# The low halves of the softmax weights: GpSimd instead of VectorE, in an attention and MoE kernel

## The chip, the core and the metric

The kernel runs on one core of one Trainium2 chip. The core has TensorE (PE: matmuls, and PEld: its weight loads), VectorE (DVE), ScalarE (ACT) and GpSimd (POOL) as compute engines, SyncE (SP), which issues nearly all DMAs here, and 16 DMA engines. Each engine works through its own instruction stream in order; semaphores tie the streams together. The metric is the device time of one execution in microseconds.

## What is computed

A local-and-global attention with ALiBi distances, followed by a two-layer feed-forward stage with a tanh-like gate:

```python
def _attn_ref(q, k, v, n_global, n_local):
    B, H, S, D = q.shape                      # 4, 8, 768, 64
    scores = np.matmul(q, k.transpose(0, 1, 3, 2)) / np.sqrt(D)
    ...
    scores = np.where(keep, scores + bias, -1e9)   # 8 global keys, 96 local ones
    a = np.exp(scores - np.max(scores, axis=-1, keepdims=True))
    a = a / (np.sum(a, axis=-1, keepdims=True) + 1e-09)
    return np.matmul(a, v)

def _moe_ref(x, w_in, w_out):                 # 3072 x 512, 512 x 2048, 2048 x 512
    h = x @ w_in
    g = h * (1.0 / (1.0 + np.exp(-1.702 * h)))
    return g @ w_out
```

The inputs and the result are float32.

## The kernel before, in words

**Numbers in two halves.** Matmuls run in float16. Each float32 operand is split into a large half, its float16 rounding, and a small half, the float16 rounding of what remains; a product is then three float16 products (large x large, large x small, small x large). Splitting is a cast, most often on ScalarE, followed by a subtraction on VectorE.

**Attention.** The 3072 tokens are 24 blocks of 128. The first four blocks (the first of each sequence) go a way of their own (`first`). The other 20 go through `unit`, four units a block with two heads each, so there are 80 units. A unit computes, for 128 queries and the 232 keys that matter to them:

1. `scores` (L536): eight matmuls into the PSUM tile `s`;
2. `rows` (L542), once a head on VectorE: adds the mask, writes the scores to the SBUF tile `p` and the row maximum to `NM`;
3. the exponential (L552), once a head on ScalarE, in place in `p`;
4. the large half (L556): ScalarE casts `p`, 128x464, into the first half of the float16 tile `hl`;
5. the small half (L557): `p` minus the large half, into the second half of `hl`;
6. a DMA transpose from `hl` to `pt` (L558), issued by SyncE;
7. `values` (L567 to L569): twelve matmuls of `pt` with the values into the PSUM tile `pv`.

There are two `hl` tiles, two `p`, four `pt`, one `s`. So unit k+2 cannot cast before the transpose of unit k has read its `hl`, nor can its row step write `p` before the subtraction of unit k has read it, and the scores of the next unit wait until both row steps of the present one have read `s`. A block's four units end in `finish`, which divides by the row sums, splits the result (L697, L699) and transposes it by DMA (L700) into `xT`.

**The feed-forward stage** runs over chunks of two blocks. The first three chunks use `up` and `down`; the other nine use `up_two` and `down_two`, a Strassen-like scheme of seven products instead of eight (`product`, L827). The gate is a tanh on ScalarE (L859) and a multiply on VectorE (L860); the result is split again (L867 on ScalarE, L868 on VectorE) and multiplied by the second weights (`pile`, L895). While one chunk is in this stage, the units of later blocks are interleaved with it.

**What sets the order.** Nothing of the order is written by hand. Each step is a task with the engines that may run it, a cost in microseconds for each, the tasks it comes after, and the tiles it uses; many have a due time. `Work.order` goes through a model time and always gives a free engine the ready task that is due first, where the tiles are free; a task with costs for two engines (for example the output copy, L907 on VectorE or L908 on ScalarE, and the cast of L697) goes to the one that ends it sooner. Due times go back from a task to those before it by their costs, and a table of small corrections by task (`NUDGE`) is added. The result is one fixed order for each engine, DMAs on SyncE included. So a changed cost or engine in one task can change the order on every engine behind it.

The small half is `t5` in `unit`; its place among the engines and its cost are the first argument of `add`.

Of the kernel before, what the change touches and what calls it, by code (L numbers as in the profile page):

```python
# [36 lines left out]
SKIP = 24  # L37
# [50 lines left out]
class Work:  # L88
# [5 lines left out]
    def add(self, on, fn, after=(), bufs=(), want=1e9):  # L94
        t = Task(on, fn, [a for a in after if a is not None], bufs, want)
        t.tag = self.tag
        for a in t.after:
            a.next.append(t)
        for b in t.bufs:
            b.users.append(t)  # L100
        self.tasks.append(t)
        return t
# [107 lines left out]
def kernel(  # L210
# [11 lines left out]
    nc = tc.nc  # L222
# [61 lines left out]
    add = wk.add  # L284
# [234 lines left out]
    def unit(n, u, want_s, want_v):  # L519

        ns = 2
        W = ns * P - SKIP
        d = blk[n]
        before = prev.get(n, blk.get(n - 1))
        sp = Buf(r_s, [P, 2, W], F32, f"s{n}_{u}")
        pr = Buf(r_pr, [P, 2, W], F32, f"p{n}_{u}")
        pt = Buf(r_pt, [P, 4 * ns, P], F16, f"pt{n}_{u}")
        hs = (2 * u, 2 * u + 1)

        def scores(e):  # L530
            for j, h in enumerate(hs):
                for s in range(ns):
                    K = (before, d)[s]["QK"]()
                    for z in range(2):
                        lo, hi = (0, P - SKIP) if s == 0 else (P - SKIP, W)
                        nc.tensor.matmul(sp()[:, j, lo:hi], d["QK"]()[:, 0, h, :], K[:, 1 + z, h, P - (hi - lo):],  # L536
                                         start=(z == 0), stop=(z == 1), skip_group_check=True)

        def rows(e, j):
            h = hs[j]  # L540
            m = mm[:, h, 0:2].rearrange("p a c -> p (a c)")[:, SKIP:]
            nc.vector.tensor_tensor_reduce(out=pr()[:, j, :], in0=sp()[:, j, :], in1=m, scale=-1.0 / SC, scalar=3.0e38,  # L542
                                           op0=ALU.add, op1=ALU.min, accum_out=NM[:, n, h:h + 1])

        t1 = add({"PE": 4 * (2 * P - SKIP) / P * MM128}, scores, [*d["qk_ready"], *before["qk_ready"], *before["G"]],
                 [sp, d["QK"], before["QK"]], want_s)
        d.setdefault("S", []).append(t1)
        ex = []
        for j in range(2):
            t2 = add({"DVE": 0.365}, lambda e, j=j: rows(e, j), [t1, M2], [sp, pr])  # L550
            checks.append(t2)
            ex.append(add({"ACT": 0.473}, lambda e, j=j: nc.scalar.activation(  # L552
                pr()[:, j, :], pr()[:, j, :], AF.Exp, bias=NM[:, n, hs[j]:hs[j] + 1], scale=-1.0,
                accum_out=d["sm"]()[:, hs[j]:hs[j] + 1]), [t2], [pr, d["sm"]]))
        hl = Buf(r_hl, [P, 2, 2, ns * P], F16, f"hl{n}_{u}", lambda t: t.rearrange("p (z a w) -> p z a w", z=2, a=2))
        t4 = add({"ACT": 0.5}, lambda e: nc.scalar.copy(hl()[:, 0, :, SKIP:], pr()), ex, [pr, hl])  # L556
        t5 = add({"DVE": 0.55}, lambda e: nc.vector.tensor_sub(hl()[:, 1, :, SKIP:], pr(), hl()[:, 0, :, SKIP:]), [t4], [pr, hl])  # L557
        t6 = add({"SP": 0.7 * ns}, lambda e: nc.sync.dma_start_transpose(pt(), hl().rearrange("p a h w -> p (a h w)")),  # L558
                 [t5], [hl, pt])

        def values(e):
            for j, h in enumerate(hs):
                o = d["pv"]()[:, h]
                for s in range(ns):
                    V = (before, d)[s]["VR"]()
                    ph, pl = pt()[:, j * ns + s, :], pt()[:, (2 + j) * ns + s, :]
                    nc.tensor.matmul(o, ph, V[:, 0, h], start=(s == 0), stop=False, skip_group_check=True)  # L567
                    nc.tensor.matmul(o, ph, V[:, 1, h], start=False, stop=False, skip_group_check=True)  # L568
                    nc.tensor.matmul(o, pl, V[:, 0, h], start=False, stop=(s == ns - 1), skip_group_check=True)  # L569

        if u == 0:
            d["pv"] = Buf(r_pv, [P, H, D], F32, f"pv{n}")
        t7 = add({"PE": 6 * ns * MM64}, values, [t6, *d["v_ready"], *before["v_ready"], *before["VG"]],
                 [pt, d["pv"], d["VR"], before["VR"]], want_v)
        d.setdefault("V", []).append(t7)
        d.setdefault("exp", []).extend(ex)
# [366 lines left out]
    for n in range(NBLK):  # L943
        c = n // 2
        wk.tag = f"prep{n}"
        if n < FIRST:
            prep_first(n)
        else:
            prep(n)
        if n < EARLY:  # L950
            own_values(n)
        if n == EARLY:
            for j in range(2):
                clear(j)
        if n >= EARLY and place(n)[1] == 1:
            wk.tag = f"over{n}"
            handover(n)
        wk.tag = f"block{n}"
        if n < EARLY:
            first(n, 8.0 + 11.0 * n)  # L960
        else:
            for u in range(NU):
                ws_ = start[c, 0] - (60.0 if c < TWO else LEAD) + 5.2 * ((n % 2) * NU + u)
                unit(n, u, ws_, ws_ + 6.0)
        leading(n)
        wk.tag = f"x{n}"
        finish(n)
# [303 lines left out]
```

## Time and profile before

| | before |
|---|---|
| time, median of 3 runs | 601.39 us (601.16 to 601.64) |
| span of the profiled execution, first to last instruction | 600.7 us |
| busy time of TensorE | 587.5 us |
| busy time of VectorE | 503.0 us |
| busy time of ScalarE | 471.4 us |
| busy time of GpSimd | 5.8 us |

The profile is of one execution, whose span of 600.7 us is 0.7 us below the median of the runs; what lies around the span is no part of it. Rows of the profile name a line of the kernel, an engine, an operation, and tiles as output<-inputs with the buffer numbers left out; then partitions x elements, the count, the busy time, the mean duration of one in ns, and the idle time of the engine ahead of it with what ended it. Matmuls overlap in the pipeline, so their single durations are longer than their spacing.

GpSimd works only at the start, on constants, an identity and a few zeroed tiles; its last instruction there starts before 7 us.

### The profile page before, as it was taken

The numbers are of one execution on the slowest core, as the hardware profiler recorded it, in microseconds if no ns is written. First come the engines' busy times: TensorE is split into PE (matmuls) and PEld (weight loads), VectorE is DVE, ScalarE is ACT, GpSimd is POOL, SyncE is SP. The second block draws the span as 40 slices with busy tenths as digits, with TensorE's granted clock in tenths as the row PEclk, the third lists the DMA queues.
The fourth block names the chain that finished last, engine by engine and source line by source line (L and its number), as shares of the span: only waits on it lengthen the run. The fifth ranks groups of instructions, "written<-read, shape, count | busy, mean of one in ns | idle before, by whom it ended". The sixth has DMA issues, their size and how long they took to land.

```text
span 600.7 us, 17037 instructions
## 1 busy us (share of the span) xinstructions
PE 587.5 (98%) x6816; PEld 445.9 (74%) x6816; DVE 503.0 (84%) x1177; ACT 471.4 (78%) x1098; POOL 5.8 (1%) x18
## 2 busy tenths in 40 slices
PE   8989999999999999999999999999999999999996
PEld 5878767777777867777677777777678768867895
DVE  6998999999999999789699789798979978766532
ACT  3878899978768988888698899788999978944432
POOL 3000000000000000000000000000000000000000
PEclk9999999999999999999999999999999999999998
DMA  8998799999976768979996999999989999920001
GB/s 225 310 251 260 227 253 198 191 179 197 212 141 128 156 117 186 196 145 196 216 206 163 226 209 238 197 233 198 236 186 223 224 193 228 234 40 3 36 1 41
DMA packets 268502, 109.58 MB, mean 182 GB/s; under 512 B 249536, under 2 KB 250048, under 8 KB 268416
## 3 DMA queue, kind: packets, MB, share of 16 engines
q1 hardware_dynamic: 267984, 108.30, 86.6%
q8 instruction: 55, 0.90, 0.7%
q14 instruction: 31, 0.25, 0.1%
q10 hardware_dynamic: 432, 0.13, 0.1%
HBM read 57.67 MB, written 6.29 MB: 106 GB/s over the span
## 4 chain that ended last, share of the span: by engine, by line
PE 85%; DMA 7%; ACT 4%; DVE 2%; issue 1%; SPq 1%; POOL 0%; DVEq 0%; ACTq 0%; POOLq 0%
PE y L895 36%; PE pa L827 14%; PE h L787 10%; PE pb L827 10%; PE s L536 5%; DMA pt<-hl 3%; DMA QK<-QK 2%; PE s L604 1%; PE pv L567 1%; PE pv L569 1%; PE pv L568 1%; PE sT L623 1%; PE idle L1060 1%; DMA xT<-x 1%; DMA out_dram<-yo 1%
## 5 line engine op out<-in xcount | busy, mean ns | idle before, releaser
L895 PE MATMUL y<-w,g 128*128 128x512 f16 (+1 forms) x1248 | 266.8, 363 | 0.0
L895 PEld LDWEIGHTS <-g 128*128 128x128 f16 x1248 | 117.9, 98 | 103.3
L827 PEld LDWEIGHTS <-w 128*128 128x128 f16 x1728 | 101.3, 98 | 5.0
L552 ACT ACTIVATE p<-p,NM 128x232 f32<-128x232 f32 x160 | 76.4, 480 | 7.0 <-DVE NM L542 7.0
L827 PEld LDWEIGHTS <-T 128*128 128x128 f16 x1296 | 77.1, 98 | 6.0
L787 PE MATMUL h<-xT,w 128*128 128x256 f16 x576 | 69.4, 273 | 0.3 <-DMA xT<-x 0.2
L542 DVE CUSTOM_DVE_ANT_0 p<-s,mm 128x232 f32<-128x232 f32 x160 | 57.7, 395 | 8.2 <-PE s L536 7.3
L787 PEld LDWEIGHTS <-w 128*128 128x128 f16 x576 | 55.2, 98 | 9.3 <-issue 0.6
L557 DVE TENSOR_TENSOR hl<-p,hl 128x464 f16<-128x464 f32 x80 | 50.9, 636 | 10.2 <-ACT hl L556 10.1
L868 DVE SCALAR_TENSOR_TENSOR g<-t,g 128x512 f16<-128x512 f32 x72 | 49.3, 687 | 11.1 <-ACT g L867 10.9
L867 ACT ACTIVATE g<-t 128x512 f16<-128x512 f32 x72 | 45.0, 628 | 9.5 <-DVE t L860 8.1
L556 ACT CAST hl<-p 128x464 f16<-128x464 f32 x80 | 46.1, 576 | 6.4 <-DMA pt<-hl 4.4
L859 ACT ACTIVATE t<-h 128x512 f32<-128x512 f32 (+1 forms) x72 | 35.9, 515 | 18.2 <-DVE h L835 15.1
L835 DVE TENSOR_TENSOR h<-pb,h 128x256 f32<-128x256 f32 x72 | 29.6, 420 | 23.0 <-PE pb L827 19.6
L827 PE MATMUL pa<-xS,T 128*128 128x128 f16 x648 | 45.0, 219 | 0.0
L860 DVE SCALAR_TENSOR_TENSOR t<-t,h 128x512 f32<-128x512 f32 (+1 forms) x72 | 38.2, 553 | 4.6 <-ACT t L859 4.0
L536 PEld LDWEIGHTS <-QK 128*128 128x128 f16 x640 | 36.5, 98 | 3.7 <-DMA QK<-QK 0.2
L536 PE MATMUL s<-QK 128*128 128x128 f16 x320 | 38.4, 219 | 0.1
L827 PE MATMUL pb<-xS,w 128*128 128x128 f16 x540 | 37.5, 219 | 0.0
L567 PE MATMUL pv<-VR,pt 128*128 128x64 f16 x288 | 34.8, 193 | 2.6 <-DMA pt<-hl 2.6
L827 PE MATMUL pa<-xT,w 128*128 128x128 f16 x540 | 37.0, 219 | 0.0
L569 PE MATMUL pv<-VR,pt 128*128 128x64 f16 x288 | 34.8, 193 | 0.0
(181 smaller groups left out, 1079.9 us busy)
## 6 DMA issues: line engine op xcount, KB each, us to landing
ws<-in_moe_w_in_dram SPq DMA_DIRECT2D x8, 1024.0 KB
ws<-in_moe_w_out_dram SPq DMA_DIRECT2D x8, 1024.0 KB
raw<-in_q_dram SPq DMA_DIRECT2D x24, 256.0 KB
raw<-in_k_dram SPq DMA_DIRECT2D x24, 256.0 KB
out_dram<-yo SPq DMA_DIRECT2D x22, 256.0 KB
QK<-QK SPq DMA_DIRECT2D x40, 128.0 KB
raw<-in_v_dram SPq DMA_DIRECT2D x20, 256.0 KB
ws_00again<-in_moe_w_in_dram SPq DMA_DIRECT2D x8, 512.0 KB
```

The costliest lines, as they stand in the source:

```text
L536: nc.tensor.matmul(sp()[:, j, lo:hi], d["QK"]()[:, 0, h, :], K[:, 1 + z, h, P - (hi - lo):], start=(z == 0), stop=(z == 1), skip_group_che ...
L542: nc.vector.tensor_tensor_reduce(out=pr()[:, j, :], in0=sp()[:, j, :], in1=m, scale=-1.0 / SC, scalar=3.0e38, op0=ALU.add, op1=ALU.min, ac ...
L552: ex.append(add({"ACT": 0.473}, lambda e, j=j: nc.scalar.activation(pr()[:, j, :], pr()[:, j, :], AF.Exp, bias=NM[:, n, hs[j]:hs[j] + 1], ...
L556: t4 = add({"ACT": 0.5}, lambda e: nc.scalar.copy(hl()[:, 0, :, SKIP:], pr()), ex, [pr, hl])
L557: t5 = add({"DVE": 0.55}, lambda e: nc.vector.tensor_sub(hl()[:, 1, :, SKIP:], pr(), hl()[:, 0, :, SKIP:]), [t4], [pr, hl])
L567: nc.tensor.matmul(o, ph, V[:, 0, h], start=(s == 0), stop=False, skip_group_check=True)
L569: nc.tensor.matmul(o, pl, V[:, 0, h], start=False, stop=(s == ns - 1), skip_group_check=True)
L787: nc.tensor.matmul(ph()[:, fi, :], w1(s, cc, z, fi), X[:, y, cc, :], start=(j + cc == 0), stop=(j == 2 and cc == NCC - 1))
L827: nc.tensor.matmul(o()[:, fi], w, x()[:, y * NCC + 2 * k + cc, t], start=(first and fi + j + cc == 0), stop=(last and j + cc == 3), skip_g ...
L867: t4 = add({"ACT": 0.53}, lambda e, g=g, tt=tt: nc.scalar.mul(g()[:, 0], tt(), SG / (SX * SW)), u, [tt, g])
L868: t5 = add({"DVE": 0.61}, lambda e, g=g, tt=tt: nc.vector.scalar_tensor_tensor(g()[:, 1], tt(), SG / (SX * SW), g()[:, 0], ALU.mult, ALU.s ...
L895: nc.tensor.matmul(y(), part(zg, f), w2(s, z, f % 2)[:, m], start=(begin and f + j == 0), stop=(end and j == 2 and f == 2 * len(steps) - 1 ...
```

## The change

The subtraction that makes the small half is issued on GpSimd, and its task says so: it may run on GpSimd alone, at a planned cost of 1.1 where VectorE's was 0.55. The instruction has the same operands and shape.

```diff
-        t5 = add({"DVE": 0.55}, lambda e: nc.vector.tensor_sub(hl()[:, 1, :, SKIP:], pr(), hl()[:, 0, :, SKIP:]), [t4], [pr, hl])
+        t5 = add({"POOL": 1.1}, lambda e: nc.gpsimd.tensor_sub(hl()[:, 1, :, SKIP:], pr(), hl()[:, 0, :, SKIP:]), [t4], [pr, hl])
```

The order changes with it from the first unit on. In the rows below, tiles carry their numbers: `p4_1` and `s4_1` belong to block 4, unit 1; `hl0` and `hl1` are the two `hl` tiles; `wa` and `w` are weights being prepared, `qk165` the halves of queries and keys of block 5.

On VectorE, at the first two units, this stood before:

```order
L370 TENSOR_SCALAR wa6_0_1052<-ws6_0_923 128x1024
L557 TENSOR_TENSOR hl0_89<-p4_0_1024,hl0_89 128x2x232
L542 ISA p4_1_1064,NM_83<-s4_1_1043,mm_91 128x232
L542 ISA NM_83 128x1
L542 ISA p4_1_1064,NM_83<-s4_1_1043,mm_91 128x232
L542 ISA NM_83 128x1
L376 ISA wa6_0_1052<-wa6_0_1052,w6_0_1036 128x2048
L456 SCALAR_TENSOR_TENSOR qk165_0_1066<-raw5_961,qk165_0_1066 128x16x64
L376 ISA wa5_1_1003<-wa5_1_1003,w5_1_966 128x2048
L557 TENSOR_TENSOR hl1_90<-p4_1_1064,hl1_90 128x2x232
```

and this stands there now:

```order
L370 TENSOR_SCALAR wa6_0_1052<-ws6_0_923 128x1024
L376 ISA wa5_1_1003<-wa5_1_1003,w5_1_966 128x2048
L542 ISA p4_1_1079,NM_83<-s4_1_1043,mm_91 128x232
L542 ISA NM_83 128x1
L542 ISA p4_1_1079,NM_83<-s4_1_1043,mm_91 128x232
L542 ISA NM_83 128x1
L376 ISA wa6_0_1052<-wa6_0_1052,w6_0_1036 128x2048
L456 SCALAR_TENSOR_TENSOR qk165_0_1065<-raw5_961,qk165_0_1065 128x16x64
```

The two subtractions are gone from the stream, and a weight step (L376 of `wa5_1`) stands in the place of the first of them, three steps earlier than it stood.

On GpSimd the whole stream behind the start is now the 80 subtractions in the order of the units; it begins so:

```order
L414 MEMSET QZ3_163 64x4x128 x2
L557 TENSOR_TENSOR hl0_89<-p4_0_1024,hl0_89 128x2x232
L557 TENSOR_TENSOR hl1_90<-p4_1_1079,hl1_90 128x2x232
L557 TENSOR_TENSOR hl0_89<-p4_2_1121,hl0_89 128x2x232
L557 TENSOR_TENSOR hl1_90<-p4_3_1167,hl1_90 128x2x232
```

Nothing else of the program stands between them, so a subtraction there follows its cast or the subtraction before it.

On SyncE, around block 9, whose keys and queries are transposed by L458 (`QK9`), this stood before (L700 is the transpose of a finished block, L397 loads, L460 a copy within `QK`):

```order
L558 DMA_TRANSPOSE pt7_2_2141<-hl0_89 128x8x128
L458 DMA_TRANSPOSE QK9_2158<-qk169_0_2040 128x16x128
L700 DMA_TRANSPOSE xT3_2203<-x166_2087 128x8x128
L558 DMA_TRANSPOSE pt7_3_2215<-hl1_90 128x8x128
L397 DMA raw10_2261<-in_q_dram 128x8x64
L460 DMA QK9_2158<-QK9_2158 64x1024 x2
```

and this stands there now:

```order
L458 DMA_TRANSPOSE QK9_2139<-qk169_0_1981 128x16x128
L558 DMA_TRANSPOSE pt7_2_2196<-hl0_89 128x8x128
L558 DMA_TRANSPOSE pt7_3_2211<-hl1_90 128x8x128
L700 DMA_TRANSPOSE xT3_2225<-x166_2111 128x8x128
L460 DMA QK9_2139<-QK9_2139 64x1024 x2
L397 DMA raw10_2265<-in_q_dram 128x8x64
```

The key transpose has moved ahead of one unit's transpose, and the transpose of the finished block behind another's.

Counted over the whole program, VectorE loses its 80 subtractions; five output copies (L908 to L907), three casts (L697) and one weight step (L374 to L373) go from ScalarE to VectorE. TensorE's instructions are the same, in another order.

## The prediction

> **What bounds the kernel now.** I read the page's busy times first, then the stretches of 60 us, then TensorE's waits, and last the path of one unit (a pair of heads of one block: scores, row maxima, exponentials, their two halves, the DMA transpose, the product with the values).
>
> ```profile
> span 600.7 us, 17037 instructions
> PE 587.5 (98%) x6816; PEld 445.9 (74%) x6816; DVE 503.0 (84%) x1177; ACT 471.4 (78%) x1098; POOL 5.8 (1%) x18
> ```
>
> TensorE is busy 98% of the span, GpSimd 1%. An average over the span hides stages, so the next view is busy time by stretch (columns: stretch, length, then busy us and instructions of PE, PEld, DVE, ACT, POOL, then TensorE's granted clock, the DMA share and GB/s):
>
> ```profile
> 60.00:120.00 60.00, 60.00 (x527) 43.82 (x526) 57.18 (x109) 56.11 (x103) 0.00 (x0) 1.00 0.99 218
> 120.00:180.00 60.00, 59.79 (x586) 42.83 (x585) 57.43 (x125) 44.88 (x104) 0.00 (x0) 1.00 1.00 183
> 180.00:240.00 60.00, 60.00 (x762) 44.81 (x761) 58.55 (x140) 51.97 (x128) 0.00 (x0) 1.00 0.75 146
> 240.00:300.00 60.00, 59.20 (x771) 44.19 (x770) 47.24 (x119) 48.87 (x126) 0.00 (x0) 1.00 0.95 187
> 300.00:360.00 60.00, 59.94 (x793) 45.62 (x791) 53.18 (x139) 53.85 (x143) 0.00 (x0) 1.00 0.95 202
> 360.00:420.00 60.00, 59.31 (x783) 44.38 (x780) 52.40 (x132) 51.62 (x133) 0.00 (x0) 1.00 1.16 216
> 420.00:480.00 60.00, 60.00 (x771) 44.66 (x769) 53.47 (x139) 56.11 (x150) 0.00 (x0) 1.00 0.99 217
> 480.00:540.00 60.00, 58.90 (x740) 43.13 (x738) 45.40 (x112) 43.95 (x116) 0.00 (x0) 1.00 0.95 176
> ```
>
> The first column of pairs is the result. Between 60 and 540 us TensorE stands idle for 0 + 0.21 + 0 + 0.80 + 0.06 + 0.69 + 0 + 1.10 = 2.86 us, at a clock of 1.00. All 80 subtractions lie in that stretch:
>
> ```profile
> L557 DVE TENSOR_TENSOR hl<-p,hl x80: 629/635/644, 82.8 to 523.8; 128x464 f16<-128x464 f32 x80
> PE pv L567 <- DMA pt<-hl: 2.6, 3, 1.1
> PE h L787 <- DMA xT<-x: 0.2, 1, 0.2
> ```
>
> The last two rows are all that TensorE's matmuls wait for from 60 to 540 us (total, times, longest), and both are DMAs. VectorE is in neither row. So 50.9 us less work on an engine that is 84% busy cannot shorten the path by itself, and the most that any reordering of this stretch can return is 2.86 us, 0.48%. After 540 us there is no subtraction, and TensorE's order there stands as before but for two neighbouring steps exchanged.
>
> **The subtraction and its price.** The removed row and the row that feeds it:
>
> ```profile
> L557 DVE TENSOR_TENSOR hl<-p,hl 128x464 f16<-128x464 f32 x80 | 50.9, 636 | 10.2 <-ACT hl L556 10.1
> ```
>
> Removed from VectorE: 80 x 0.636 = 50.9 us. On GpSimd the trace shows nothing of the kind. The nearest rows of its own are these:
>
> ```profile
> L252 POOL MEMSET idle<- 128x512 bf16 x1 | 0.5, 525 | 0.3 <-POOLq L1253 0.3
> masks.py:199 POOL TENSOR_SCALAR_AFFINE_SELECT ident<-ident 128x128 f32<-128x128 f32 x1 | 0.3, 294 | 0.0
> L1021 POOL MEMSET ones<- 128x1 f32 x1 | 0.1, 99 | 0.0
> ```
>
> The lower end is the memset, which reads nothing: 525 x 464 / 512 = 0.48 us. The select is the only one that reads a tensor: beyond the 0.099 us of a one-element memset it spends 0.195 us on 128 elements, 1.52 ns each, so 464 elements cost 0.099 + 0.71 = 0.81 us. The subtraction reads two tensors; if the second costs as much again, the upper end is 0.099 + 1.41 = 1.51 us. I take 1.15, between the last two, since the select is the nearest row. The Trainium skill, GPSIMD Engine Reference, section "Elementwise — side-by-side cycle accounting", gives 4497 ns for a two-input add of 2048 elements a partition; an estimate by that page is 464 / 2048 of it, 1.02 us, and the sum below would be the same within 0.3 us.
>
> **The chain of one unit.** This is the timeline around one unit in steady state (start, duration, engine, line):
>
> ```profile
> 253.33 0.28 PE L536 MATMUL s<-QK 128*128 128x128 f16 x2
> 253.64 0.40 DVE L542 CUSTOM_DVE_ANT_0 p<-s,mm 128x232 f32<-128x232 f32 x1
> 256.01 0.58 ACT L556 CAST hl<-p 128x464 f16<-128x464 f32 x1
> 256.75 0.64 DVE L557 TENSOR_TENSOR hl<-p,hl 128x464 f16<-128x464 f32 x1
> 257.41 1.27 SPq L558 DMA_TRANSPOSE pt<-hl  x1
> 264.07 0.19 PE L567 MATMUL pv<-VR,pt 128*128 128x64 f16 x1
> ```
>
> Scores end at 253.61, the transpose is issued at 257.41, 3.80 us later, and the values' first product starts at 264.07, 6.66 us behind the issue, without a wait. The large half ends at 256.59 and VectorE takes up the small half at 256.75: 0.16 us is queueing behind VectorE's other work, which the new engine does not have. So the issue moves by 1.15 - 0.64 - 0.16 = +0.35 us (from -0.3 with the memset's price to +0.7 with 1.51). What hides it is the lead that the program's order gives each unit: the TensorE work that stands between its scores and its values. I counted it through both orders for all 80 units, with the matmuls at their spacing in the chain of waits:
>
> ```profile
> 201.20 1.34 PE pa L827 x24
> 203.56 2.59 PE y L895 x12
> ```
>
> The rows give 0.056 us for a 128-column and 0.216 us for a 512-column matmul. The mean lead is 11.7 us before and 12.1 after: the new order gives back about what the slower engine takes. Units with under 9.5 us of lead were 8 and are 6. So I cost the longer chain at nothing. If that cover is gone (1.51 us a subtraction), the units with under 10 us of lead, 14 in the new order, wait some 0.35 us more each, +5 us; that is its upper end. Behind the issue stand SyncE's other DMAs, which move with it, because SyncE issues in order.
>
> **The transposes that TensorE does wait for** are those that land late:
>
> ```profile
> 288.71 6.49 DMA pt<-hl
> 402.00 6.64 DMA pt<-hl
> 477.75 7.87 DMA pt<-hl
> ```
>
> Three of 80 units wait, 0.7 to 1.1 us each, because issue to landing took 6.5 to 7.9 us there against under 6.66 in the unit above. Which transposes meet a full queue follows from the order on SyncE, and that is new from the first unit on. The same number of meetings elsewhere would cost the same; but 80 units, 20 key transposes and all the reloads are dealt anew, and only three bad meetings is close to the best deal, so a loss is likelier than a gain. I take +1 us, with ends -2.6 (none left) and +4 (seven of them).
>
> **Where VectorE is on TensorE's path.** The scores' PSUM tile has one buffer, so the next scores wait for the last row maximum. Where two units follow closely, little is left:
>
> ```profile
> 231.88 0.41 DVE L860 SCALAR_TENSOR_TENSOR t<-t,h 128x256 f32<-128x256 f32 x1
> 232.53 0.39 DVE L542 CUSTOM_DVE_ANT_0 p<-s,mm 128x232 f32<-128x232 f32 x1
> 233.03 0.26 PE L536 MATMUL s<-QK,QK 128*128 128x104 f16 x2
> ```
>
> The second row ends at 232.92 and the next scores start at 233.03: 0.11 us of slack. Of the 79 successive pairs, counted in the timeline, 13 have 0.42 us or less, 0.3 in the middle. Anything that holds VectorE up ahead of such a row is paid by TensorE at once. Does GpSimd hold VectorE up? No row shows both at work (POOL 0.00 in every stretch above), so the price is bounded: 0 if the engines do not meet, and a whole subtraction, 1.15 us, if one excludes the other and VectorE always comes second. I take the middle, 0.57 us for each subtraction. If half of the 13 tight places are hit, they pay 6.5 x (0.57 - 0.3) = 1.8 us. In the stretch from 180 to 240 us VectorE is busy 58.55 of 60:
>
> ```profile
> 180.00:240.00 60.00, 6.98 (x11) 1.00 0.75 146
> ```
>
> That row is the subtractions alone: 6.98 us leave, and 11 x 0.57 = 6.3 us come back, so the fullest stretch stays as full as it was; I add 0.5 us. With the whole price 12.7 come back, 5.7 more than left against 1.45 us of room.
>
> **The sum**, against the profiled execution's own 600.7 us (the median of the runs, 601.4, has some 0.7 us around it): VectorE's relief 0, longer chain 0, new meetings of the transposes +1, tight places +1.8, the full stretch +0.5: 600.7 + 3.3 + 0.7 = **604.7 us**.
>
> **Rivals.**
> (1) *The engines exclude each other fully, and VectorE is the one that waits.* For it: many of VectorE's instructions read two SBUF tensors, as the subtraction does,
>
> ```profile
> L868 DVE SCALAR_TENSOR_TENSOR g<-t,g 128x512 f16<-128x512 f32 x72 | 49.3, 687 | 11.1 <-ACT g L867 10.9
> L456 DVE SCALAR_TENSOR_TENSOR qk<-raw,qk 128x1024 f16<-128x1024 f32 x20 | 24.4, 1220 | 1.4 <-ACT qk L455 1.3
> ```
>
> so a subtraction seldom finds 1.15 us without one of them. Against it: outside 60 to 240 us VectorE has 6.5 to 14.6 us of room in each 60. Price: 13 x (1.15 - 0.3) = 11 us at the tight places if all are hit, 5.5 for half; 5.7 - 1.45 = 4.2 in the full stretch; +1 for the transposes: about 11 us, 612. It decides from some 0.9 us of hold a subtraction upwards. The Trainium skill states this rule: SBUF — State Buffer, "Who interferes with whom", says that a VectorE instruction with two SBUF inputs and a GpSimd instruction that reads SBUF shut each other out for a whole instruction, and that the one issued first goes first. No run here shows it yet.
> (2) *Everything is hidden.* The leads swallow the slower engine, no tight place is hit, and the new meetings cost what the old ones did: 601.4. For it: TensorE's whole wait is now 2.86 us although landing times vary by over a microsecond.
> (3) *The new order is lucky.* VectorE's relief, less the few copies that the new order moves to it from ScalarE, lets the halves be issued sooner and the three waits go: at best 601.4 - 2.9 = 598.5.
>
> **How the numbers follow.** About 0.2%, 1.2 us, is what a measurement of this kernel can tell from no change. The forecast (a loss of 1.2 to 8 us) gets 0.5, rival 1 gets 0.15, rival 2 0.24, rival 3 0.11. So slower 0.65, within 0.24, faster 0.11. The range runs from 600.2, which keeps rival 2 and leaves most of rival 3 out, to 612, which takes rival 1 in up to its price.
>
> **What would show it.** GpSimd's row L557 at 0.9 to 1.5 us, 80 times; VectorE's busy time down by 40 to 50 us, or less where its rows have become longer than the 687 and 1220 ns above (a hold shows as longer rows or as idle time ahead of them). The loss as new waits of TensorE from 60 to 540 us, at L567 for transposes and at L536 for row maxima. Rows at unchanged length would speak against any meeting of the two engines; no new TensorE wait would make the forecast wrong. A GpSimd row of 2 us or more would make every unit's lead too short, and the loss would pass 612.

## The result, and the profile after

| | before | after |
|---|---|---|
| time, median of 4 runs each | 601.51 us (601.16 to 602.01) | 616.85 us (614.68 to 617.06) |
| ratio | | 1.0239, 95% interval 1.0214 to 1.0264 |
| span of the profiled execution | 600.7 us | 615.1 us |

The changed kernel is slower by 15.3 us. The forecast was 3.3 us slower, with a range that ended at 612.0. The direction was right, the size was not. All runs behind this document were undisturbed but one of e10 below (613.69 us, in a slower state), which is left out of its median and ratio.

First the head of the page of the changed kernel, then its subtraction on GpSimd, from the view of that line (min/median/max in ns) and from the page:

```profile
span 615.1 us, 17165 instructions
PE 589.6 (96%) x6814; PEld 445.6 (72%) x6816; DVE 494.6 (80%) x1106; ACT 466.5 (76%) x1089; POOL 100.5 (16%) x98
```

```profile
L557 POOL TENSOR_TENSOR hl<-p,hl x80: 1063/1071/2071, 82.6 to 537.3; 128x464 f16<-128x464 f32 x80
...
L557 POOL TENSOR_TENSOR hl<-p,hl 128x464 f16<-128x464 f32 x80 | 94.8, 1185 | 437.0 <-ACT hl L556 382.3
```

TensorE's busy time rose by 2.1 us and the span by 14.4, so nearly all of the loss is TensorE standing idle. The subtraction takes 1.07 us alone, close to the 1.15 taken; the mean is 1.185, and the longest took 2.07, so GpSimd's own rows are held up too. VectorE is busy 8.4 us less, not 40 to 50 less. Part of that is work which the new order brings it from ScalarE; the larger part is that some of its own rows have become longer. The groups of VectorE's instructions by form (busy time and mean ns of one), after and then before:

```profile
L868 DVE SCALAR_TENSOR_TENSOR g<-t,g 128x512 f16<-128x512 f32 x72 | 54.3, 756 | 15.9 <-ACT g L867 15.6
L860 DVE SCALAR_TENSOR_TENSOR t<-t,h 128x512 f32<-128x512 f32 x36 | 27.0, 749 | 7.2 <-ACT t L859 6.3
...
L542 DVE CUSTOM_DVE_ANT_0 p<-s,mm 128x232 f32<-128x232 f32 x160 | 57.1, 391 | 10.8 <-PE s L536 10.5
L835 DVE TENSOR_TENSOR h<-pb,h 128x256 f32<-128x256 f32 x72 | 29.1, 418 | 27.1 <-PE pb L827 19.9 <-ACT qk L455 2.6 <-ACT h L832 2.5
```

```profile
L860 DVE SCALAR_TENSOR_TENSOR t<-t,h 128x512 f32<-128x512 f32 x36 | 24.7, 687 | 4.3 <-ACT t L859 3.8
...
L542 DVE CUSTOM_DVE_ANT_0 p<-s,mm 128x232 f32<-128x232 f32 x160 | 57.7, 395 | 8.2 <-PE s L536 7.3
L835 DVE TENSOR_TENSOR h<-pb,h 128x256 f32<-128x256 f32 x72 | 29.6, 420 | 23.0 <-PE pb L827 19.6
```

L868 went from 687 to 756 ns, L860 from 687 to 749: both read two tensors from SBUF. L542 and L835, which read one of their two inputs from PSUM (`s`, `pb`), stayed where they were. Each VectorE row that started behind 75 us and took over 0.06 us more than the median of its form before, counted one by one, gives 57 rows with 30.6 us more in all, 0.38 us for each of the 80 units, and never over 0.90 us in one row. A stretch of the timeline of the changed kernel shows how that comes about (start, duration, engine, line; in brackets the idle time of the engine ahead of it and what ended it):

```profile
173.66 0.69 DVE L466 SCALAR_TENSOR_TENSOR VRover<-over,VRover 128x512 f16<-128x512 f32 x1
173.96 1.30 POOL L557 TENSOR_TENSOR hl<-p,hl 128x464 f16<-128x464 f32 x1 [6.72 <-ACT hl L556]
174.26 2.09 DVE L757 TENSOR_TENSOR T<-t,T 128x1024 f16<-128x1024 f32 x1
176.27 0.68 DVE L797 SCALAR_TENSOR_TENSOR t<-t,h 128x512 f32<-128x512 f32 x1
176.87 1.21 DVE L757 TENSOR_TENSOR T<-t,T 128x1024 f16<-128x1024 f32 x1
178.00 0.68 DVE L799 SCALAR_TENSOR_TENSOR g<-t,g 128x512 f16<-128x512 f32 x1
178.60 2.34 DVE L733 TENSOR_TENSOR t<-w 128x1024 f32<-128x1024 f16 x2
180.87 0.38 DVE L542 CUSTOM_DVE_ANT_0 p<-s,mm 128x232 f32<-128x232 f32 x1
...
181.64 0.27 PE L536 MATMUL s<-QK,QK 128*128 128x104 f16 x2 [1.88 <-DVE NM L542]
```

The subtraction starts while L466 runs and takes 1.30 us, some 0.23 longer than alone; it ends at 175.26. The L757 that starts meanwhile is on record with 2.09 us where its twin at 176.87 takes 1.21: 0.88 us more, of the 1.00 that the subtraction still had to run. All that stands behind it on VectorE moves by as much, down to the row maximum, and there TensorE waits 1.88 us for its next scores. But the hold isn't all of it. Two long weight sums (L733, 2.34 us together) and eight other steps, five of them in these rows, stand between the last row step and this one, and that is the order's doing; before, TensorE waits for no row maximum at all. Both causes meet in this one place.

The windows of the changed kernel (columns as before) and its TensorE waits from 60 to 560 us:

```profile
60.00:120.00 60.00, 60.00 (x527) 43.73 (x526) 57.83 (x102) 55.31 (x104) 11.64 (x8) 1.00 0.94 218
120.00:180.00 60.00, 58.41 (x559) 40.97 (x556) 58.06 (x110) 40.91 (x92) 12.07 (x10) 1.00 0.88 176
180.00:240.00 60.00, 54.11 (x685) 40.03 (x686) 49.43 (x115) 46.78 (x116) 11.78 (x10) 1.00 0.76 136
240.00:300.00 60.00, 59.17 (x777) 44.47 (x775) 49.34 (x122) 50.09 (x133) 11.99 (x11) 1.00 0.87 179
300.00:360.00 60.00, 58.13 (x758) 43.65 (x756) 47.09 (x115) 50.67 (x127) 10.21 (x9) 1.00 0.98 197
360.00:420.00 60.00, 59.68 (x766) 44.32 (x764) 50.51 (x126) 52.00 (x139) 12.71 (x11) 1.00 1.12 223
420.00:480.00 60.00, 56.32 (x730) 42.01 (x729) 48.38 (x113) 50.14 (x128) 10.64 (x9) 1.00 0.90 190
480.00:540.00 60.00, 59.86 (x793) 45.48 (x791) 45.78 (x117) 51.50 (x141) 13.71 (x12) 1.00 1.13 220
```

```profile
PE s L536 <- DVE NM L542: 5.3, 5, 1.9
PE pv L567 <- DMA pt<-hl: 2.0, 3, 1.0
PE pb L827 <- DVE xS L723: 1.5, 1, 1.5
PE pb L827 <- DVE h L835: 1.3, 1, 1.3
PE s L536 <- DMA QK<-QK: 1.0, 1, 1.0
PE pa L827 <- ACT h L843: 0.8, 1, 0.8
PE pb L827 <- ACT h L832: 0.7, 2, 0.4
PE pa L827 <- DVE h L835: 0.6, 1, 0.6
PE y L895 <- DVE g L799: 0.6, 1, 0.6
```

Idle time of TensorE from 60 to 540 us went from 2.86 to 14.32 us: 11.5 of the span's 14.4, and 5.89 of them between 180 and 240. Of the 13.8 us in the list of waits, VectorE is waited for in 9.3, in a kernel where it has less to do. The transposes, which were 2.6, are 2.0.

### The profile page after: what moved, and what is told of

It reads as the page before. It is cut to its first block, busy times and chain, and to the rows that moved or that the text cites. A ratio compares the mean times of both kernels' runs of the same rounds, so it can differ in the third digit from the quotient of the medians.

```text
span 615.1 us, 17165 instructions
## 1 busy us (share of the span) xinstructions
PE 589.6 (96%) x6814; PEld 445.6 (72%) x6816; DVE 494.6 (80%) x1106; ACT 466.5 (76%) x1089; POOL 100.5 (16%) x98
## 4 chain that ended last, share of the span: by engine, by line
PE 55%; DVE 18%; ACT 12%; DMA 7%; issue 5%; SPq 2%; DVEq 0%; ACTq 0%
PE y L895 24%; PE pa L827 9%; PE pb L827 7%; PE h L787 6%; PE s L536 3%; DVE p L542 2%; ACT p L552 2%; ACT junk L404 2%; DMA pt<-hl 2%; DMA ws_11again<-in_moe_w_out_dram 1%; PE s L604 1%; PE sT L623 1%; DVE T L757 1%; ACT hl L556 1%; DMA QK<-QK 1%
## 5 line engine op out<-in xcount | busy, mean ns | idle before, releaser
L557 POOL TENSOR_TENSOR hl<-p,hl 128x464 f16<-128x464 f32 x80 | 94.8, 1185 | 437.0 <-ACT hl L556 382.3
L868 DVE SCALAR_TENSOR_TENSOR g<-t,g 128x512 f16<-128x512 f32 x72 | 54.3, 756 | 15.9 <-ACT g L867 15.6
L542 DVE CUSTOM_DVE_ANT_0 p<-s,mm 128x232 f32<-128x232 f32 x160 | 57.1, 391 | 10.8 <-PE s L536 10.5
L835 DVE TENSOR_TENSOR h<-pb,h 128x256 f32<-128x256 f32 x72 | 29.1, 418 | 27.1 <-PE pb L827 19.9
L860 DVE SCALAR_TENSOR_TENSOR t<-t,h 128x512 f32<-128x512 f32 (+1 forms) x72 | 40.4, 583 | 10.2 <-ACT t L859 9.3
```

Of the source, the lines that this page charges most:

```text
L557: t5 = add({"POOL": 1.1}, lambda e: nc.gpsimd.tensor_sub(hl()[:, 1, :, SKIP:], pr(), hl()[:, 0, :, SKIP:]), [t4], [pr, hl])
L860: return add({"DVE": 0.08 + 0.265 * w}, lambda e: nc.vector.scalar_tensor_tensor(o(), o(), 1.0, src(), ALU.add, ALU.mult), [t1], srcs)
L868: t5 = add({"DVE": 0.61}, lambda e, g=g, tt=tt: nc.vector.scalar_tensor_tensor(g()[:, 1], tt(), SG / (SX * SW), g()[:, 0], ALU.mult, ALU.s ...
```

## The experiments

Each group below asks one question. Behind each time stands its ratio to the kernel before, timed beside it (medians of 602.2 to 603.1 us), with the 95% interval; the ratio is estimated from all the runs and can differ by some 0.1% from the quotient of the two medians. Differences between two experiments are taken between their ratios where the kernel before was timed anew. Letters in the expectations name the theories that were open at the time.

**Is it the engine or the order?** Two kernels separate them. e1 keeps the order before exactly, on every engine, and lets GpSimd execute the subtraction:

```diff
-        t5 = add({"DVE": 0.55}, lambda e: nc.vector.tensor_sub(...
+        t5 = add({"DVE": 0.55}, lambda e: nc.gpsimd.tensor_sub(...
```

> The order of before on every engine, but each of the 80 subtractions is issued on GpSimd at the place where VectorE had it; the planner does not know. Theory A (the new order costs most of the 15 us: it deals the tight places and the transposes anew, while GpSimd's rows themselves hold VectorE for some 29 us that mostly fall beside other work): this kernel is near before, 602 to 607 us. Theory B (the meeting of the two engines and the later small half cost most of it, whatever the order): 612 to 620 us. VectorE's own rows should be lengthened by 20 to 40 us in total under both.

e2 has the order of the changed kernel, with the subtraction executed on VectorE (against the changed kernel):

```diff
-        t5 = add({"POOL": 1.1}, lambda e: nc.gpsimd.tensor_sub(...
+        t5 = add({"POOL": 1.1}, lambda e: nc.vector.tensor_sub(...
```

> The order of after on every engine, but the subtractions are issued on VectorE, where the order puts them; GpSimd does nothing. No two engines meet at SBUF, and VectorE carries 50.9 us more than the order was made for. Theory A (the order): 610 to 618 us, TensorE still waits for row maxima (L536) and products. Theory B (the meeting): 601 to 606 us.

Measured: e1 604.99 us, ratio 1.0042 (1.0026 to 1.0058), so 2.5 us over the kernel before. e2 616.14 us, ratio 1.0217 (1.0190 to 1.0243), so 13.7 us, with no subtraction on GpSimd. Both lie in the ranges of theory A. (TensorE's clock was 0.993 to 0.995 in the four runs of e2 against 0.996 to 1.000 after; by that difference of some 0.4%, an estimate, 2.5 us of its time may be the clock.) The hold is there in e1 as it is after: the group of L868 in e1,

```profile
L868 DVE SCALAR_TENSOR_TENSOR g<-t,g 128x512 f16<-128x512 f32 x72 | 55.2, 769 | 19.7 <-ACT g L867 18.8
```

is even a little longer than after (756), and the one-by-one count gives 28.5 us against 30.6. So about the same held time, together with the later small half, costs 2.5 us in the old order. The timeline of e2 at the place shown above:

```profile
178.41 0.63 DVE L557 TENSOR_TENSOR hl<-p,hl 128x464 f16<-128x464 f32 x1
178.96 1.22 DVE L757 TENSOR_TENSOR T<-t,T 128x1024 f16<-128x1024 f32 x1
...
184.70 0.39 DVE L542 CUSTOM_DVE_ANT_0 p<-s,mm 128x232 f32<-128x232 f32 x1
...
185.48 0.27 PE L536 MATMUL s<-QK,QK 128*128 128x104 f16 x2 [1.59 <-DVE NM L542]
```

Here VectorE spends 0.63 us on the subtraction, in place of the 0.88 for which it was held, and TensorE waits 1.59 us in place of 1.88. At this place the order, planned as if this time were free, loses by either use of it.

**Is it the table of corrections?** `NUDGE` was written for the old order, and could simply not fit the new. e3 empties it in the kernel before, e4 in the changed kernel, e10 in e1 (`NUDGE = {}` is the whole edit).

> Before with the table of corrections to due times emptied, so its order is the planner's own. Theory A, in its form 'the table was fitted to one order and is worth some 10 us there': 608 to 616 us. Theory B: within 3 us of before, 601 to 604 us.

> After with the table of corrections emptied. Theory A in that form: about as long as before without the table (within 4 us of e3_no_table_before). Theory B: 12 us or more above e3_no_table_before.

> The order of e3_no_table_before (booked on VectorE at 0.55, no table), the subtraction issued on GpSimd: e1 once more in another order. Theory D: e3_no_table_before plus 2 to 3 us, 605 to 609 us. Theory L: 610 us or more.

Measured: e3 604.71 us, 1.0026 (0.9997 to 1.0054); e4 616.79 us, 1.0241 (1.0214 to 1.0268); e10 605.61 us, 1.0050 (1.0028 to 1.0073). e3 lies 0.7 us beyond the range of theory B, and its interval holds 1, so no loss of its own is shown; e4 lies in theory B's range. The change costs nearly as much without the table (616.79 - 604.71 = 12.1 us) as with it. The table isn't the cause. e10, in the range of theory D, lies 0.24% or 1.4 us over e3, less than e1's 2.5, but with intervals that overlap.

**What is the meeting of the two engines worth in the new order?** e5 keeps the changed kernel's order, and keeps GpSimd at work about as long in each unit, but with next to no reading. The small halves are left out: the tile is filled with zeros but for its first column.

```diff
-        t5 = add({"POOL": 1.1}, lambda e: nc.gpsimd.tensor_sub(hl()[:, 1, :, SKIP:], pr(), hl()[:, 0, :, SKIP:]), [t4], [pr, hl])
+        t5 = add({"POOL": 1.1}, lambda e: [nc.gpsimd.tensor_sub(hl()[:, 1, :, SKIP:SKIP + 1], pr()[:, :, 0:1], hl()[:, 0, :, SKIP:SKIP + 1]),
+                                           nc.gpsimd.memset(hl()[:, 1, :, SKIP:], 0.0), nc.gpsimd.memset(hl()[:, 1, 0, SKIP:], 0.0),
+                                           nc.gpsimd.tensor_sub(hl()[:, 1, :, SKIP:SKIP + 1], pr()[:, :, 0:1], hl()[:, 0, :, SKIP:SKIP + 1])], [t4], [pr, hl])
```

> The order of after on every engine, and GpSimd is held about as long for each unit, but it nearly reads nothing: the subtraction is made for one column of each head only, before and after two memsets of the small half (so the small halves are left out of the result). Theory C (the order of after counts on VectorE time that the meeting with GpSimd's reads takes away; the order of before does not, since the subtraction's old place is a hole in it): without the reads VectorE's rows keep their length and the time falls to 601 to 606 us. Theory A (the order is bad by itself, on any machine): it stays at 612 to 618 us.

Measured: 610.32 us, 1.0123 (1.0104 to 1.0142), between the ranges of both theories. The page of e5:

```profile
L557 POOL TENSOR_TENSOR hl<-p,hl 128x2 f16<-128x2 f32 x160 | 54.9, 343 | 398.2 <-ACT hl L556 391.6
...
L557 POOL MEMSET hl<- 128x464 f16 (+1 forms) x160 | 63.2, 395 | 9.3
...
L868 DVE SCALAR_TENSOR_TENSOR g<-t,g 128x512 f16<-128x512 f32 x72 | 49.4, 688 | 16.5 <-ACT g L867 16.3
```

GpSimd worked 54.9 + 63.2 = 118.1 us on this step, more than the 94.8 of the real subtraction, and VectorE's L868 is back at 688 ns: the memsets, which read nothing, don't hold up VectorE's rows with two inputs from SBUF. Counted as before, five rows are longer, by 1.0 us in all; each reads one tensor and overlaps a memset. At the place shown above the timeline of e5 has

```profile
172.29 1.22 DVE L757 TENSOR_TENSOR T<-t,T 128x1024 f16<-128x1024 f32 x1
...
179.76 0.26 PE L536 MATMUL s<-QK,QK 128*128 128x104 f16 x2
```

with L757 at 1.22 us and no wait of TensorE behind the same two weight sums: here it took the order and the hold together. Of the 9.1 us that TensorE does wait in e5 from 60 to 560 us, 4.3 are for DMAs (2.2 of them for transposes), 3.2 for VectorE and 1.6 for ScalarE; before, it was 2.8 us, all for DMAs. Four of the rows:

```profile
PE s L536 <- DVE NM L542: 1.7, 4, 0.7
PE pb L827 <- DVE xS L723: 1.5, 1, 1.5
PE s L536 <- DMA QK<-QK: 1.2, 2, 0.9
PE pa L827 <- ACT h L843: 0.9, 1, 0.9
```

The reading adds to this mainly at VectorE: 9.3 us of waits for it in the changed kernel against 3.2. So in the new order the reading costs the difference of the ratios 1.0239 and 1.0123, 1.2% or 7 us, and the order without it costs 1.2%, again 7 us. Up to 1 us of the reading's price may be the clock (0.996 to 1.000 against 0.999 to 1.000); the two profiled executions, both at 1.000, are 615.1 and 608.8 us long, 6.3 apart. (A unit's step takes 1.48 us in e5 against 1.185; if that costs anything, the order costs less and the reading more.)

e11 goes at the length of a hold: e1 with the subtraction in two pieces of 128x232.

```diff
+        t5 = add({"DVE": 0.55}, lambda e: [nc.gpsimd.tensor_sub(hl()[:, 1, j, SKIP:], pr()[:, j], hl()[:, 0, j, SKIP:]) for j in range(2)], [t4], [pr, hl])
```

> e1_engine_only with each subtraction made in two pieces, one a head, 128x232 each. If the hold of a whole instruction is what e1 loses its 2.5 us by, shorter holds cost less, 602 to 604 us; if the later small half is, the second fixed cost makes it longer, 605 to 608 us.

Measured: 609.01 us, 1.0099 (1.0077 to 1.0120), worse than e1 and past both ranges. A piece takes 0.629 us (median), so two take 1.26 against 1.07; with the time that GpSimd is itself held up a unit's two pieces take 1.59 us in the mean, against 1.19 in e1. The time that VectorE is held falls from 28.5 to 23.3 us, and yet TensorE waits longer for transposes from 60 to 560 us than in e1 (1.2 us, three times):

```profile
PE pv L567 <- DMA pt<-hl: 3.3, 6, 0.9
```

Shorter holds bought nothing. The order is that of before, so its price is not set by the held time alone: this speaks for the later small half as a second cost. How e1's 2.5 us divide between the two isn't shown.

**Is the plan's idea of the time to blame?** Four kernels change only planned numbers, or who may do the work. e6: the changed kernel, with the hold reserved on VectorE by planning each row step longer. e7: the kernel before, VectorE still subtracting, planned at what the hold takes. e8: the changed kernel, planned as if GpSimd were as fast as VectorE was. e9: GpSimd subtracts, but the plan keeps a longer VectorE step for it. e12: the planner may choose the engine; it put 18 of the 80 on GpSimd.

```diff
# e6
-            t2 = add({"DVE": 0.365}, lambda e, j=j: rows(e, j), [t1, M2], [sp, pr])
+            t2 = add({"DVE": 0.545}, lambda e, j=j: rows(e, j), [t1, M2], [sp, pr])
# e7, e8, e9 and e12, in this order
+        t5 = add({"DVE": 0.19}, lambda e: nc.vector.tensor_sub(...
+        t5 = add({"POOL": 0.55}, lambda e: nc.gpsimd.tensor_sub(...
+        t5 = add({"DVE": 1.1}, lambda e: nc.gpsimd.tensor_sub(...
+        t5 = add({"DVE": 0.55, "POOL": 1.1}, lambda e: ENG[e].tensor_sub(...
```

> After, with 0.18 more planned for each of a unit's two row steps on VectorE (0.36 a unit, which is what the lengthened rows of after come to: 28.7 us over 80), everything else as it is. The order then leaves VectorE room for the meeting. Theory C: 602 to 608 us. Theory A (luck of the deal): no reason to improve, 610 to 620 us.

> Before, with the subtraction on VectorE, but planned at 0.19 instead of 0.55: an order that counts on 28.8 us of VectorE time that is not there, with GpSimd idle and no two engines meeting. Theory C: it loses as after does, 609 to 618 us, with TensorE waiting for row maxima and products between 120 and 210 us. Theory A (loss belongs to orders made for GpSimd, or to luck): 600 to 607 us.

> After, with the subtraction planned at 0.55 on GpSimd instead of 1.1: another order, with VectorE as free in the plan as in after, and the small half promised half a microsecond too early. If the planned length of the small half (due times moved ahead by 0.55) made the order bad: 601 to 607 us. Theory C: VectorE is promised just as much, 610 to 620 us.

> The subtraction runs on GpSimd, but the planner still books it on VectorE, at 1.1: a new order with the length of the small half right and 1.1 of VectorE time kept free behind each cast, where the two engines may meet. Theory D (an order is good when it keeps VectorE free while GpSimd reads; e1 was good for that reason and not because it is the order of before): 602 to 608 us. Theory L (e1 was good because the order of before is): 610 to 618 us, like the other new orders.

> The planner may put each subtraction on VectorE (0.55) or GpSimd (1.1), whichever ends it sooner by its times; 18 of 80 go to GpSimd. Theory D: VectorE's time is booked for most units, 600 to 606 us. TensorE's waits before were 2.9 us, so 598 is the floor; a version faster than before would have to come from here.

| | median us | ratio (95%) | in the range of |
|---|---|---|---|
| e6 | 614.08 | 1.0185 (1.0165 to 1.0205) | theory A |
| e7 | 607.63 | 1.0079 (1.0053 to 1.0104) | neither |
| e8 | 615.79 | 1.0207 (1.0187 to 1.0228) | theory C |
| e9 | 619.00 | 1.0269 (1.0239 to 1.0300) | neither |
| e12 | 607.62 | 1.0072 (1.0048 to 1.0096) | past theory D's |

Halving the planned length on GpSimd brings little, if anything (e8). Time reserved for the hold wins back some 0.5% of 2.4 (e6). e7 has everything on VectorE, and an order that counts on 28.8 us of VectorE that are not there: it costs 0.8%, less than theory C had it. e12 holds VectorE for 10.9 us only and costs 0.7%; its order is another new one. e9 missed its expectation: with 1.1 us a unit on VectorE the plan has 44 us more of that engine than before, and the order that results is a third one and worse still, so it says nothing for or against the hold. No version came down to the kernel before.

**Is it one bad place?** In the changed kernel the last weight transform (`twist` for the fourth pair of weight blocks, L733 to L769) has moved ahead of the first chunk's half sums (`sums`, L720 to L723), and both use the two `wa` tiles: L720 starts at 191.57 there, in a stretch where TensorE loses 5.89 us. e13 gives that transform an earliest time in the plan; e14 does it in e5; e15 moves that transform early in the kernel before, by an entry `"T3": -20.0` in `NUDGE` (the four are counted from 0); e16 is e15 with the subtraction on GpSimd as in e1.

```diff
# e13, e14
-            t.soon = 0.0
+            t.soon = 0.0 if S < 3 else 180.0
# e15, e16
-NUDGE = {"T2": -1.5, "down02": 1.4, ...
+NUDGE = {"T2": -1.5, "T3": -20.0, "down02": 1.4, ...
```

In e14 the small halves are left out as in e5. In e15 and e16 the third transform comes behind the fourth, and reads the weights of block 5 after the fourth has written its own result over them, so these two compute that part of the product from other numbers, with the same instructions.

> After, with one line more: the last of the four weight transforms (twist 3, lines L733 to L769) may not be planned before 180 in model time. In after it stands ahead of the first chunk's sums (L720 to L723) on VectorE and holds both tiles they share; here the sums stand first, as in before. Theory O (that inversion is what the new order costs by itself, and the meeting of the engines adds the rest): the 7.3 us that after loses from 170 to 215 us fall to 2 or less, the time to 608 to 612 us. Theory N (no single place, the order is worse all over): 613 to 618 us.

> The same order as e13_twist_held, with GpSimd held by memsets as in e5_no_reads (small halves left out of the result). Theory O: both causes are gone, 602 to 606 us. Theory N: near e5_no_reads, 609 to 611 us.

> Before, everything on VectorE, with the last weight transform's due time moved 20 earlier in the table, so that it stands ahead of the first chunk's sums as in after. Theory O: the inversion alone costs VectorE's old kernel some 4 to 8 us, 606 to 610 us, with TensorE waiting between 170 and 215 us at L536 and L827. Theory N: within 3 us of before.

> The order of e15_twist_early_before with the subtraction issued on GpSimd in its place. Theory O with a meeting that costs the same in any order: e15_twist_early_before plus 2 to 3 us. If the meeting costs more where the order leaves less slack: plus 5 us or more.

| | median us | ratio (95%) |
|---|---|---|
| e13 | 616.24 | 1.0235 (1.0202 to 1.0268) |
| e14 | 611.04 | 1.0144 (1.0126 to 1.0162) |
| e15 | 608.48 | 1.0090 (1.0070 to 1.0109) |
| e16 | 611.04 | 1.0139 (1.0120 to 1.0158) |

e13 and e14 take that place away (L720 starts at 178.5 in e13, ahead of the last transform) and win nothing, as theory N had it. e15 lost 6 us, which is theory O's number, but it doesn't test that theory: it exchanges the third and the fourth transform, so three of them stand ahead of the half sums as before, and L720 starts at 179.7 us against 179.6 before, not 12 us later as after. Its loss is the price of one more new order. The waits of TensorE in e13 from 60 to 560 us show where the loss went:

```profile
PE s L536 <- DVE NM L542: 7.8, 8, 2.5
...
PE pb L827 <- DVE xS L723: 0.6, 1, 0.6
```

The wait for the half sums fell from 1.5 to 0.6 us, and the waits for row maxima rose from 5.3 to 7.8. The loss moved from one step of VectorE's stream to the next. With e13 the theory of one bad place fell. What stands of the other two is that e16 lies 2.6 us over e15, the price that e1 shows over the kernel before.

**Does any new order cost as much?** e5 loses 7 us by its order alone. e17 and e18 are the kernel before with all the work where it was, and about a tenth less or more planned for the subtraction on VectorE, which is enough to deal the order anew:

```diff
-        t5 = add({"DVE": 0.55}, lambda e: nc.vector.tensor_sub(...
+        t5 = add({"DVE": 0.50}, ...      # e17; 0.60 in e18
```

> The kernel before, VectorE still making the small halves, with 0.50 in place of 0.55 us planned for one. The work and the engines are those of before; only the order is made anew. Theory P (any order made anew from other numbers loses, because the order of before is a good one among many): 604.5 to 610, with waits of PE for row maxima or in front of the half-sum products that the kernel before doesn't have. Theory Q (the loss comes from the time that the plan takes off VectorE; here it is 80 x 0.05 = 4 us of it in place of 44): 601.5 to 603.5.

> The kernel before, VectorE still making the small halves, with 0.60 in place of 0.55 us planned for one, so the plan has 4 us more of VectorE than before. Theory P: 604.5 to 610, as with 0.50. Theory Q: 600.5 to 602.5, no loss, since no time is taken off VectorE.

Measured: e17 605.23 us, 1.0039 (1.0017 to 1.0060); e18 605.72 us, 1.0068 (1.0045 to 1.0090). Both are slower, e18 although it books more of VectorE's time, and both medians lie in the range of theory P. TensorE's waits in e17, 60 to 560 us:

```profile
PE pv L567 <- DMA pt<-hl: 2.3, 5, 0.7
PE s L536 <- DVE NM L542: 1.1, 2, 0.8
PE pb L827 <- DVE xS L723: 0.4, 1, 0.4
```

The last two are kinds of waits that the changed kernel has, in small: none for a row maximum or a half sum is there before. (e18 waits 0.6 us for half sums and for no row maximum.) So a plan that is changed by a tenth in one number cost 0.4 and 0.7%, 2.4 and 4 us; the order before is better than both of these. With e7 (0.8%) and e15 (0.9%) there are four new orders with all the work on VectorE, and they cost 2.4 to 5.4 us.

## Why the forecast was wrong, point by point

**The subtraction's own price** was right: 1.07 us alone against 1.15 taken, inside the bounds. The estimate from the Trainium skill (GPSIMD Engine Reference, "Elementwise — side-by-side cycle accounting"), 1.02 us, was nearer still. (By it the tight places would have come to 6.5 x (0.51 - 0.3) = 1.4 us and the sum to 0.4 us less, not within 0.3.)

**The longer chain at nothing** fits the changed kernel, where TensorE's waits for transposes are 2.0 us in three places and were 2.6 in three. In the old order e11 speaks for a cost once the small half comes still later. The reason given for the three waits before, late landing, isn't borne out by the rows beside it: 6.49 and 6.64 us lie under the 6.66 of the unit that didn't wait.

**The meeting of the engines, tight places +1.8 and full stretch +0.5**, was right in kind. For the old order the size came out too, 2.5 us in e1 for the sum of 2.3, but that is partly luck: the hold is 0.36 us a unit there and not 0.57, and TensorE waits for a row maximum in two places (1.3 us), not in six or seven. In the new order, which is the one that the forecast was for, the reading cost 7 us where 2.3 were put: the tight places had been counted in the order of before, and the hold of 0.38 us a unit met another set of them (counted in the timelines, the next scores start within 0.1 us of the last row maximum in 8 of the 79 pairs after and in 4 in e5, in none before). The trace agrees with the rule of the Trainium skill (SBUF — State Buffer, "Who interferes with whom"): rows with two SBUF inputs are held, L542 and L835 with a PSUM input are not, the subtraction itself is held when it comes second (2.07 us at the longest), and memsets leave rows with two SBUF inputs at their length (e5). Rival 1, which took this rule at its full price of a whole subtraction with VectorE always second, had the mechanism but not its price: the hold never reached the 0.9 us a subtraction from which it was to decide, and its 612 was near the result for a reason that the runs don't bear out.

**The new order, +1 for "new meetings of the transposes" with ends at -2.6 and +4**, is the step that failed. The order was weighed by the leads from scores to values and by SyncE's queue alone, as if a new order could add waits for DMAs only. Measured: 7 us for the order with hardly any reading (e5: 1.0104 to 1.0142). For DMAs TensorE waits 4.3 us there against 2.8 before, 1.5 more and close to the +1; what the term left out are waits for VectorE and ScalarE, none before and 4.8 us in e5. In part they follow from row steps and half sums that now come behind weight sums and transforms, which the plan had put into the freed time. Other new orders, with all the work left on VectorE, cost 2.4 to 5.4 us (e7, e15, e17, e18), so a part of the 7 is what a new deal of this planner costs at all.

**The terms were added as if the price of a hold were the same in every order.** The time for which VectorE is held is about the same in every order: 28.5 us in e1, 30.2 in e10 (against e3), 27.9 in e16, 30.6 after, 31.8 in e13. The price of the reading isn't:

| order | held, us | price of the reading |
|---|---|---|
| before (e1 over before) | 28.5 | 0.4%, 2.5 us |
| e10 over e3 | 30.2 | 0.2%, 1.4 us |
| e16 over e15 | 27.9 | 0.5%, 2.6 us between the medians |
| e13 over e14 | 31.8 | 0.9%, 5 us |
| after (over e5) | 30.6 | 1.2%, 7 us |

The first and the last row are clear of each other; the intervals of those between overlap. A reading that fits them: in the three orders whose plan still counted the subtraction on VectorE, taking it away left gaps that swallowed most of the hold; in the two planned for GpSimd the gaps had been filled with other steps, and the hold went through to TensorE. It fits the place at 174 us too; that it is the reason elsewhere is an inference. It doesn't explain e11, which has the old order and less held time and costs 1.0%, and the first three rows contain the later small half as well, which the last two don't.

**"At most 2.86 us can be gained"** wasn't tested, since no run gained anything: of the eighteen kernels none had a median below that of the one before.

What stays open: whether the order planned for GpSimd, which costs 2 to 5 us more than the four other new orders, is worse by its plan or only the worst of a few draws. It isn't the table (e4), the planned length (e8) or the one inversion (e13), and reserving the held time brings back only a part (e6). Also 2.9 us of the span's difference lie outside 60 to 540 us; TensorE's busy time in the first 60 us is 53.91 us after against 55.02, but it is 54.05 in e15 and 54.03 in e11 too, whose orders there are that of the kernel before, so that part of it is probably no effect of the change.

## What to carry to other kernels

Where one planner sets the order on all engines, a changed cost is two changes, the work and a new order: run the new engine in the old order and the old engine in the new order before believing either, and deal the order anew by a trifle to learn what a new order costs by itself. Moving work off an engine that TensorE didn't wait for bought nothing here, and the relief was spent twice: the planner filled it with other steps, and GpSimd's reads took over half of it back by holding VectorE up. If such a move must be made, try it with the order held fixed; here that lost 2.5 us instead of 15. And count tight places in the order that will run: those of the old order say little about the new.

## What was not expected of the hardware

Rows with a single SBUF input were held as well. The copy L483 in the changed kernel, and in the kernel before:

```profile
L483 DVE COPY QK<-KG x16: 179/188/1056, 92.3 to 515.1; 128x128 f16<-128x128 f16 x16
```

```profile
L483 DVE COPY QK<-KG x16: 185/190/192, 93.8 to 500.5; 128x128 f16<-128x128 f16 x16
```

A copy of 0.19 us took up to 1.06, over five times its length, and two of the casts of L697 that run on VectorE (0.42 us) took 0.68 and 0.81 longer. The Trainium skill (SBUF — State Buffer, "Who interferes with whom") states this of copies and casts in a mode that uses both ports; the trace agrees in the effect and doesn't show the mode. A memset was enough for that: the five longer rows in e5 are two of these copies, a cast of L697 and one step each of L370 and L373, and that cast, which has only memsets beside it, took 0.68 us in place of 0.42. The short instructions are held for as long as the long ones, so they lose the most in proportion. And small pieces on GpSimd are dear: a one-column subtraction took 0.206 us (median), half the tensor 0.629 and the whole 1.07, so some 0.19 us of each instruction is not the elements.
